# Spreading a bonus vector and loading weights without GpSimd, in a fused RWKV-6 and token-mixing kernel

## The chip, the cores and the metric

The kernel runs on one core of one Trainium2 chip. The metric is device time in microseconds. Before the change the median of three runs is 148.23 us (146.26 to 151.97).

## What is computed

Two stages follow each other. The first is a linear attention with a decaying state (batch 4, 8 heads, sequence 768, head size 48); the second mixes tokens with two projections and a last matrix product. Cut to what matters:

```python
for t in range(S):                       # S = 768, state is D x D per batch and head
    cur = einsum('bhd,bhe->bhde', u * k_t, v_t)      # u: the bonus vector, heads x D
    y_t = einsum('bhd,bhde->bhe', r_t, state + cur)
    state = w_t[..., None] * state + einsum('bhd,bhe->bhde', k_t, v_t)
x = y as (B, S, H*D)                     # H*D = 384
W_tok = (x @ w_q) @ (x @ w_k)^T / sqrt(64)
out = relu(W_tok @ x) @ w_out            # w_q, w_k: 384 x 64; w_out: 384 x 384
```

All inputs and the output are fp32.

## The kernel before

The sequence is cut into units ("tiles") of 256 tokens. There are 12: three for each of four batches, numbered n = 0 to 11. A tile holds 128 partitions with two tokens each, 8 heads and 48 elements. For each tile these steps are made (the name of the step is that of its function):

- `load` (L134, SP queue): w, k, r, v, 384 KB each, in three buffers per tensor.
- `log` (L139, ACT): logarithm of w. `sums` (PE): running sums of it by triangular matrices, into PSUM tiles `cw`. `expk` (L159, ACT) writes `em`, `expr` (L166, ACT) works on `cw` in place, `decay` (L173, ACT) writes `pt`.
- `rdec` (L182, DVE, two instructions) writes RdS = r times a decay. `kdec` (L189, POOL) writes KdS = k times `em`. `trR` transposes both on PE into `psT`; `evT` (L209, DVE) copies `psT` to RKT.
- `amat` (PE) and `mask` (L226, DVE, two instructions): the masked score matrix AmB.
- The bonus term is apart from it: `uk1` (L232, POOL) is k times `ubc`, the bonus vector u spread over all 128 partitions; `uk2` (L239, POOL) multiplies by r; `red` (L246, DVE) sums per head to `diag`; `vd` (L253, POOL) is V times `diag`; `vswap` (L260, SP queue) moves it into the token order of the output, Vn. `vcast` (L193, ACT) is the cast of v to V.
- `state`, `stadd` (PE), `stev` (L289, DVE): the state SB. `ymat`, `yst` (PE), `yev` (L325, DVE): X = Y + Vn.
- `xtr` (PE), `xev` (L341, ACT), `qkmat` (PE), `qkev` (L361 and L362, ACT): the projections of x.

After three tiles a batch is complete, and `tmat`, `tev` (L375), `mix`, `mixev` (L387), `fin`, `finev` (L404 on ACT, L406 on DVE) and `store` (L411, ACT queue) make its output. All matmuls are issued through one helper at L58.

The order of the work on each engine isn't left to a scheduler. Each step has a due time in a list (`steps`, and `bsteps` for a batch), tile n is displaced by n times P = 7.42, and all steps of all tiles are sorted by that time and written out in this order. Each engine works through its own part of it in order; an instruction that waits holds all behind it on its engine.

`uload` and `wload` are due first of all. `uload` (L450, L451) loads u into one partition over the SP queue, and GpSimd's partition broadcast spreads it to `ubc`. `wload` (L454 to L456) issues three transfers on GpSimd's queue: the query weights stay fp32 (`wq_f`), the key weights and the output weights are cast to bf16 by the transfer. `wcast` (L460, ACT) casts and scales the query weights after the first tiles' activations.

Of the kernel before, what the change touches and what calls it, by code (L numbers as in the profile page):

```python
# [11 lines left out]
F32 = mybir.dt.float32  # L12
# [6 lines left out]
def _rep(ap, axis, n):  # L19
    a = [list(x) for x in ap.ap]  # L20
    a.insert(axis, [0, n])
    return dataclasses.replace(ap, ap=a)
# [3 lines left out]
def kernel(  # L26
# [12 lines left out]
    nc = tc.nc  # L39
    B, H, S, D = r.shape  # L40
    C = 128
# [7 lines left out]
    DM = H * D  # L49
    DH = moe_w_q.shape[1]  # L50
    NK = DM // 128
# [15 lines left out]
    consts = ctx.enter_context(tc.tile_pool(name="consts", bufs=1))  # L67
# [14 lines left out]
            lst.append(consts.tile([C, 2, NP, C], BF16, name=f"{nm}{i}", tag=f"{nm}{i}"))  # L82
        PT.append(consts.tile([C, 2, H], F32, name=f"pt{i}", tag=f"pt{i}"))

    u1 = consts.tile([1, DM], F32, tag="u1")
    ubc = consts.tile([C, DM], F32, tag="ubc")
    wq_sb = consts.tile([128, NK, DH], BF16, tag="wq")
    wk_sb = consts.tile([128, NK, DH], BF16, tag="wk")
    wout_sb = consts.tile([128, NK, DM], BF16, tag="wo")
    wq_f = consts.tile([128, NK, DH], F32, tag="wqf")  # L90

    ld = ctx.enter_context(tc.tile_pool(name="ld", bufs=3))
    hw = ctx.enter_context(tc.tile_pool(name="hw", bufs=3))
# [24 lines left out]
    def at(t, fn):  # L118
        plan.append((t, len(plan), fn))
# [10 lines left out]
    def load(n, nm, ap):  # L130
        b, m = divmod(n, NU)
        src = ap[b, :, ds(m * C2, C2)]
        t = ld.tile([C, H, D2], F32, name=nm + "G", tag=nm + "G")
        nc.sync.dma_start(out=t, in_=src.rearrange("h (p j) d -> p h (j d)", j=2))  # L134
        T[nm, n] = t
# [311 lines left out]
        nc.vector.memset(PT[i], 0.0)  # L447

    def uload():
        nc.sync.dma_start(out=u1, in_=u.rearrange("h d -> (h d)"))  # L450
        nc.gpsimd.partition_broadcast(ubc, u1)  # L451

    def wload():
        nc.gpsimd.dma_start(out=wq_f, in_=moe_w_q.rearrange("(n p) h -> p n h", p=128))  # L454
        nc.gpsimd.dma_start(out=wk_sb, in_=moe_w_k.rearrange("(n p) h -> p n h", p=128))
        nc.gpsimd.dma_start(out=wout_sb, in_=moe_w_out.rearrange("(n p) d -> p n d", p=128))  # L456

    def wcast():
        T["wq"] = wq_sb
        nc.scalar.activation(wq_sb, wq_f, ACT.Copy, bias=0.0, scale=scale)  # L460

    P = 7.420616340685398
    steps = [
        (-6.28, log, ()),
        (2.72, uk1, ()),
        (2.75, uk2, ()),
        (3.11, sums, ()),
        (3.14, expk, ()),  # L470
        (3.14, expr, ()),
        (3.14, decay, ()),
        (4.39, rdec, ()),
        (6.88, kdec, ()),
        (8.86, vcast, ()),
        (9.54, trR, (0, )),
        (9.99, red, ()),
        (10.19, trR, (1, )),
        (10.98, evT, ()),
        (11.01, amat, (0, )),  # L480
        (12.45, mask, (0, )),
        (13.24, vd, ()),
        (13.27, vswap, ()),
        (14.3, amat, (1, )),
        (14.33, mask, (1, )),
        (16.24, state, ()),
        (16.65, stadd, (0, )),
        (16.68, stev, (0, )),
        (17.69, stadd, (1, )),
        (17.87, stev, (1, )),  # L490
        (17.98, ymat, ()),
        (18.01, yst, ()),
        (18.47, yev, ()),
        (20.81, xtr, ()),
        (22.26, xev, ()),
        (23.63, qkmat, ()),
        (24.22, qkev, ()),
    ]
    bsteps = [
        (-0.35, tmat, ()),  # L500
        (1.14, tev, ()),
        (2.14, mix, (0, )),
        (2.29, mixev, (0, )),
        (3.11, mix, (2, )),
        (3.65, mix, (1, )),
        (6.35, mixev, (1, )),
        (6.78, mixev, (2, )),
        (7.16, mix, (3, )),
        (8.18, mixev, (3, )),
        (9.78, mix, (5, )),  # L510
        (10.47, mixev, (5, )),
        (11.93, mix, (4, )),
        (11.97, mixev, (4, )),
        (12.0, fin, (0, )),
        (12.38, finev, (0, 0, )),
        (12.57, fin, (1, )),
        (12.76, finev, (1, 1, )),
        (14.6, store, (0, )),
        (15.74, fin, (2, )),
        (15.77, finev, (2, 0, )),  # L520
        (16.04, fin, (3, )),
        (16.1, fin, (5, )),
        (17.73, fin, (4, )),
        (17.82, finev, (4, 0, )),
        (18.28, finev, (3, 1, )),
        (19.09, finev, (5, 1, )),
        (19.92, store, (1, )),
        (20.86, store, (2, )),
    ]
    for n in range(NT):  # L530
        t0 = n * P
        tl = t0 - 3 * P + 9.67 if n >= 3 else n - 100
        for i, (nm, ap) in enumerate((("w", w), ("k", k), ("r", r), ("v", v))):
            at(tl + 0.01 * i, lambda n=n, nm=nm, ap=ap: load(n, nm, ap))
        for dt, fn, a in steps:
            if fn in (stadd, stev) and n % NU == NU - 1 and a == (1,):
                continue
            at(t0 + dt, lambda n=n, fn=fn, a=a: fn(n, *a))
        if n % NU == NU - 1:
            b = n // NU  # L540
            tb = t0 + 25.81
            for dt, fn, a in bsteps:
                at(tb + dt, lambda b=b, fn=fn, a=a: fn(b, *a))
    at(-99.995, uload)
    at(-98.995, wload)
    at(12.49573647335233, wcast)
    with tc.manual_schedule():
        for _, _, fn in sorted(plan, key=lambda x: x[:2]):
            fn()
# [30 lines left out]
```

## Time and profile before

The profile is of one execution on the chip.

| | |
|---|---|
| median of three runs | 148.23 us |
| the profiled execution's own time | 150.44 us |
| its span, first to last instruction | 148.7 us |
| busy: PE | 100.9 us (68%) |
| busy: DVE | 92.5 us (62%) |
| busy: POOL (GpSimd) | 88.1 us (59%) |
| busy: ACT | 81.8 us (55%) |
| moved by DMA | 26.66 MB, mean 179 GB/s |

PE is TensorE, PEld its weight loads, DVE VectorE, ACT ScalarE, POOL GpSimd, SP the engine that issues most transfers; a q behind a name (SPq, POOLq) is its issue of transfers. In a group such as `KdS<-kG,em`, the tile before the arrow is written from those behind it. The bracket at the end of a line of the timeline is the engine's idle time before it, and what ended it; "issue" means that the engine waited for nothing that the profile shows. The page divides the span into 40 equal slices of 3.7 us and gives for each the busy share of an engine in tenths.

### The profile page before, as it was taken

Reading aid. Unit: us, or ns where it says so; the run is one execution under the profiler, and the core shown is the slowest. Engines: PE = TensorE matmul, PEld = TensorE weight load, DVE = VectorE, ACT = ScalarE, POOL = GpSimd, SP = SyncE. Lnnn points to the kernel's source line nnn. Section 1 sums busy time; section 2 is a strip of 40 time slices with the busy share of each in tenths; the row PEclk is TensorE's granted clock in tenths of the full one; section 3 lists DMA queues with packets and bytes.
Section 4 is the critical chain, followed back from the end, with each engine's and each line's share of the span. In section 5 each row is a group of like instructions: output and inputs, shape, how many; then the busy total and the mean of one; then the engine's idle time right before and its main releaser. Section 6 shows DMA issues by size and latency. Waiting matters only on the chain. (4 is left out here: it accounts for less than half of the span.)

```text
span 148.7 us, 4118 instructions
## 1 busy us (share of the span) xinstructions
PE 100.9 (68%) x1684; PEld 66.7 (45%) x1684; DVE 92.5 (62%) x138; ACT 81.8 (55%) x174; POOL 88.1 (59%) x85
## 2 busy tenths in 40 slices
PE   0603000046797969689999899898989997986930
PEld 0202000033645746465767566464756564653410
DVE  5002000045769889898899896997989989760210
ACT  3235400008267376768897777498856782645520
POOL 7603400899999597989596987949596803000000
PEclk9999999999997899999999999999999999999695
DMA  4999990019298949679796967969856310248074
GB/s 115 298 270 309 309 194 0 0 26 293 60 281 231 321 127 285 182 193 271 188 235 173 324 181 226 296 173 246 221 134 166 109 40 4 53 110 212 0 198 119
DMA packets 58084, 26.66 MB, mean 179 GB/s; under 512 B 51505, under 2 KB 58034, under 8 KB 58066
## 3 DMA queue, kind: packets, MB, share of 16 engines
q1 hardware_dynamic: 53762, 21.24, 54.1%
q10 hardware_dynamic: 3456, 4.72, 11.6%
q0 software_dynamic: 848, 0.44, 2.0%
q8 instruction: 13, 0.21, 0.6%
q14 instruction: 5, 0.04, 0.1%
HBM read 19.66 MB, written 4.72 MB: 164 GB/s over the span
## 5 line engine op out<-in xcount | busy, mean ns | idle before, releaser
L159 ACT ACTIVATE em<-cw,bias 128x384 bf16<-128x384 f32 x24 | 12.8, 577 | 29.2 <-PE cw L58 29.2
L226 DVE TENSOR_TENSOR AmB<-A,MASK 128x1024 bf16<-128x1024 f32 x24 | 28.5, 1217 | 0.3 <-PE A L58 0.2
L253 POOL TENSOR_TENSOR Vd<-V,diag 128x768 bf16<-128x768 bf16 x12 | 17.7, 1474 | 17.9 <-DVE diag L246 12.8
L232 POOL TENSOR_TENSOR uk<-kG,ubc 128x768 f32<-128x768 f32 x12 | 21.7, 1809 | 9.6 <-issue 9.6
L239 POOL TENSOR_TENSOR uk<-uk,rG 128x768 f32<-128x768 f32 x12 | 21.7, 1810 | 0.9
L246 DVE TENSOR_REDUCE diag<-uk 128x16 f32<-128x768 f32 x12 | 11.3, 945 | 16.8 <-POOL uk L239 16.8
L58 PEld LDWEIGHTS <-KdS 64*128 64x128 bf16 (+1 forms) x256 | 11.6, 104 | 22.2 <-POOL KdS L189 17.7
L58 PE MATMUL psT<-ID,KdS 128*128 128x128 bf16 x96 | 8.3, 237 | 17.4 <-POOL KdS L189 17.4
L189 POOL TENSOR_TENSOR KdS<-kG,em 128x768 bf16<-128x768 f32 x12 | 19.6, 1636 | 0.3 <-ACT em L159 0.2
L182 DVE TENSOR_TENSOR RdS<-rG,cw 128x384 bf16<-128x384 f32 x24 | 12.1, 547 | 10.8 <-ACT cw L166 10.8
L58 PE MATMUL fps<-wout_sb,mixT 128*128 128x384 bf16 x72 | 15.4, 356 | 1.2 <-ACT osb L404 1.1
L139 ACT ACTIVATE logw<-wG 128x768 bf16<-128x768 f32 x12 | 10.1, 842 | 10.9 <-DMA wG<-in_w_dram 10.7
L325 DVE TENSOR_TENSOR X<-Y,Vn 128x768 bf16<-128x768 f32 x12 | 11.5, 958 | 7.3 <-PE Y L58 4.0
L209 DVE COPY RKT<-psT 128x2048 bf16<-128x2048 bf16 x12 | 14.6, 1216 | 1.7 <-PE psT L58 1.7
L58 PE MATMUL cw<-logw,BI 128*128 128x384 bf16 x36 | 11.4, 374 | 4.9 <-ACT logw L139 4.9
L58 PE MATMUL psT<-ID,RdS 128*128 128x128 bf16 x96 | 8.8, 241 | 7.6 <-DVE RdS L182 5.8
L289 DVE TENSOR_TENSOR SB<-Sn,pt 128x384 bf16<-128x384 f32 x20 | 11.1, 554 | 4.0 <-PE Sn L58 2.9
L387 ACT ACTIVATE mixT<-mps 128x384 bf16<-128x384 f32 x24 | 10.7, 493 | 4.6 <-PE mps L58 4.4
L341 ACT COPY XT<-xt_ps 128x768 bf16<-128x768 bf16 x12 | 9.6, 799 | 6.0 <-PE xt_ps L58 6.0
L58 PEld LDWEIGHTS <-RKT 48*64 48x64 bf16 (+1 forms) x464 | 10.3, 108 | 4.9 <-issue 2.6
L166 ACT ACTIVATE cw<-cw,bias 128x384 f32<-128x384 f32 x24 | 12.3, 558 | 0.2
L406 DVE COPY osb<-fps 128x384 f32<-128x384 f32 x12 | 6.6, 552 | 8.8 <-ACT mixT L387 5.0
(62 smaller groups left out, 172.3 us busy)
## 6 DMA issues: line engine op xcount, KB each, us to landing
wG<-in_w_dram SPq DMA_DIRECT2D x12, 384.0 KB, 5.0
kG<-in_k_dram SPq DMA_DIRECT2D x12, 384.0 KB, 5.2
rG<-in_r_dram SPq DMA_DIRECT2D x12, 384.0 KB, 5.6
vG<-in_v_dram SPq DMA_DIRECT2D x12, 384.0 KB, 5.8
out_dram<-osb ACTq DMA_DIRECT2D x24, 192.0 KB, 2.9
Vn<-Vd SPq DMA_DIRECT2D x48, 48.0 KB, 2.5
wout_sb<-in_moe_w_out_dram POOLq DMA_DIRECT2D x1, 288.0 KB, 6.6
wq_f<-in_moe_w_q_dram POOLq DMA_DIRECT2D x1, 96.0 KB, 5.1
```

Of the source, the lines that this page charges most:

```text
L58: nc.tensor.matmul(o, l, rr, start=start, stop=stop, skip_group_check=True, is_transpose=trans)
L159: nc.scalar.activation(em[:, j], T["cw", n, 1 + j][:, 0:DM], ACT.Exp, bias=bias[2 + j], scale=-1.0)
L166: nc.scalar.activation(cw, cw, ACT.Exp, bias=bias[j], scale=1.0)
L182: nc.vector.tensor_tensor(pad(Rd)[:, j], jhd(T["r", n])[:, j], T["cw", n, j][:, 0:DM].rearrange("p (h d) -> p h d", d=D), ALU.mult)
L189: nc.gpsimd.tensor_tensor(pad(T["Kd", n]), jhd(T["k", n]), hd(T["em", n]), ALU.mult)
L209: nc.vector.tensor_copy(RKT, T["psT", n])
L226: nc.vector.tensor_tensor(T["AmB", n][:, js].rearrange("p q h t -> p h q t"), T["A", n, js], _rep(_rep(MASK[:, js], 1, NP), 1, 2), ALU.mult)
L232: nc.gpsimd.tensor_tensor(uk, T["k", n].rearrange("p h (j d) -> p h j d", j=2), _rep(ubc.rearrange("p (h d) -> p h d", d=D), 2, 2), ALU.mult)
L239: nc.gpsimd.tensor_tensor(uk, uk, T["r", n].rearrange("p h (j d) -> p h j d", j=2), ALU.mult)
L246: nc.vector.tensor_reduce(diag.rearrange("p j h -> p h j"), T["uk", n], axis=AX.X, op=ALU.add)
L253: nc.gpsimd.tensor_tensor(Vd, T["V2", n], _rep(T["diag", n], 3, D), ALU.mult)
L325: nc.vector.tensor_tensor(T["X", b][:, ds(2 * m, 2)], T["Y", n][:, :, 0:DM], T["Vn", n], ALU.add)
```

## The change

The bonus vector is read by a transfer whose source repeats the 1536 bytes 128 times, so that it lands in all partitions; it is issued on the ACT queue ahead of the first `log`. The partition broadcast, and the one-partition tile u1, are gone. The three weights are loaded in fp32 on the ACT queue, due right after the first `log`, and ScalarE casts all three in `wcast`. The due times of nearly all steps are new; P is the same.

```diff
-    u1 = consts.tile([1, DM], F32, tag="u1")
+    wk_f = consts.tile([128, NK, DH], F32, tag="wkf")
+    wout_f = consts.tile([128, NK, DM], F32, tag="wof")
...
     def uload():
-        nc.sync.dma_start(out=u1, in_=u.rearrange("h d -> (h d)"))
-        nc.gpsimd.partition_broadcast(ubc, u1)
+        uf = u.rearrange("h d -> (h d)")
+        nc.scalar.dma_start(out=ubc, in_=_rep(uf, 0, C))

     def wload():
-        nc.gpsimd.dma_start(out=wq_f, in_=moe_w_q.rearrange("(n p) h -> p n h", p=128))
-        nc.gpsimd.dma_start(out=wk_sb, in_=moe_w_k.rearrange("(n p) h -> p n h", p=128))
-        nc.gpsimd.dma_start(out=wout_sb, in_=moe_w_out.rearrange("(n p) d -> p n d", p=128))
+        for t, a in ((wq_f, moe_w_q), (wk_f, moe_w_k), (wout_f, moe_w_out)):
+            nc.scalar.dma_start(out=t, in_=a.rearrange("(n p) h -> p n h", p=128))

     def wcast():
         T["wq"] = wq_sb
         nc.scalar.activation(wq_sb, wq_f, ACT.Copy, bias=0.0, scale=scale)
+        nc.scalar.copy(wk_sb, wk_f)
+        nc.scalar.copy(wout_sb, wout_f)
...
-        (-6.28, log, ()),
-        (2.72, uk1, ()),
-        (2.75, uk2, ()),
-        (3.11, sums, ()),
+        (-7.73, log, ()),
+        (-2.67, uk1, ()),
+        (1.48, sums, ()),
...
-        (6.88, kdec, ()),
-        (8.86, vcast, ()),
+        (4.93, uk2, ()),
+        (6.95, vcast, ()),
+        (7.29, kdec, ()),
...
-        (13.24, vd, ()),
-        (13.27, vswap, ()),
+        (12.04, vd, ()),
...
+        (14.71, vswap, ()),
...
-        tl = t0 - 3 * P + 9.67 if n >= 3 else n - 100
+        tl = t0 - 3 * P + 9.92 if n >= 3 else n - 100
...
-            tb = t0 + 25.81
+            tb = t0 + 24.41
...
-    at(-98.995, wload)
-    at(12.49573647335233, wcast)
+    at(-5.674325351920891, wload)
+    at(12.474566743711435, wcast)
```

On GpSimd this gives, for the first tiles, the order uk1(0), uk1(1), uk2(0), kdec(0), vd(0), uk1(2), uk2(1), kdec(1), vd(1), and so on; before it was uk1(0), uk2(0), kdec(0), uk1(1), uk2(1), vd(0), kdec(1), uk1(2), uk2(2), vd(1), kdec(2). The order of DVE's instructions is the same but for two swapped pairs of a mask and an output copy. On PE the `mix` and `fin` matmuls of a batch stand at other places between the tiles' matmuls. On ACT the `log` of a later tile and `vcast` change places.

More of the change, by code (lines that the diff above doesn't have):

```diff
@@ L460, in wcast @@
         nc.scalar.activation(wq_sb, wq_f, ACT.Copy, bias=0.0, scale=scale)
+        nc.scalar.copy(wk_sb, wk_f)
+        nc.scalar.copy(wout_sb, wout_f)
     P = 7.420616340685398
     steps = [
-        (-6.28, log, ()),
-        (2.72, uk1, ()),
-        (2.75, uk2, ()),
-        (3.11, sums, ()),
[L470 to L473, printed above, removed]
-        (6.88, kdec, ()),
-        (8.86, vcast, ()),
[L476 to L481, printed above, removed]
-        (13.24, vd, ()),
-        (13.27, vswap, ()),
[L484 to L497, printed above, removed]
+        (-7.73, log, ()),
+        (-2.67, uk1, ()),
+        (1.48, sums, ()),
+        (1.75, expk, ()),
+        (1.81, expr, ()),
+        (1.83, decay, ()),
+        (2.25, rdec, ()),
+        (4.93, uk2, ()),
+        (6.95, vcast, ()),
+        (7.29, kdec, ()),
+        (7.68, trR, (0, )),
+        (7.7, trR, (1, )),
+        (8.31, red, ()),
+        (8.67, evT, ()),
+        (9.5, amat, (0, )),
+        (11.63, mask, (0, )),
+        (12.04, vd, ()),
+        (12.63, amat, (1, )),
+        (12.66, mask, (1, )),
+        (14.53, state, ()),
+        (14.71, vswap, ()),
+        (14.96, stadd, (0, )),
+        (14.99, stev, (0, )),
+        (15.71, stadd, (1, )),
+        (15.74, stev, (1, )),
+        (16.59, ymat, ()),
+        (16.62, yst, ()),
+        (16.65, yev, ()),
+        (19.34, xtr, ()),
+        (19.87, xev, ()),
+        (21.93, qkmat, ()),
+        (22.64, qkev, ()),
     ]
@@ L500 @@
         (-0.35, tmat, ()),
-        (1.14, tev, ()),
+        (-0.32, tev, ()),
         (2.14, mix, (0, )),
-        (2.29, mixev, (0, )),
-        (3.11, mix, (2, )),
+        (2.33, mixev, (0, )),
         (3.65, mix, (1, )),
+        (4.58, mix, (2, )),
         (6.35, mixev, (1, )),
[L507 to L512, printed above, removed]
+        (6.64, mixev, (2, )),
+        (7.42, mix, (3, )),
+        (7.45, mixev, (3, )),
+        (9.08, mix, (5, )),
+        (9.81, mixev, (5, )),
+        (11.34, mix, (4, )),
         (11.97, mixev, (4, )),
-        (12.0, fin, (0, )),
-        (12.38, finev, (0, 0, )),
+        (12.34, fin, (0, )),
+        (12.37, finev, (0, 0, )),
         (12.57, fin, (1, )),
-        (12.76, finev, (1, 1, )),
+        (12.6, finev, (1, 1, )),
         (14.6, store, (0, )),
@@ L522 @@
         (16.1, fin, (5, )),
[L523 to L526, printed above, removed]
+        (17.36, finev, (3, 1, )),
+        (18.76, fin, (4, )),
+        (19.11, finev, (4, 0, )),
+        (19.14, finev, (5, 1, )),
         (19.92, store, (1, )),
```

## The prediction

> **What bounds the kernel now.** I read the page's 40 slices first. From slice 5 to 8 (18.6 to 31 us) every compute engine stands at or near 0, and afterwards DVE shows 8 or 9 to slice 34. So there are two stages: a start with a hole in it, and a steady run. The chain that ended last is of little use: it reaches back only to 134.8 us, the last matmuls and stores. So next come the stretches of time; columns are length, then busy time and count of each engine, TensorE clock, DMA share, GB/s.
>
> ```profile
> 6.40:13.60 7.20, 1.42 (x13) 0.54 (x11) 1.03 (x2) 3.14 (x7) 0.01 (x1) 1.00 1.07 286
> 13.60:16.80 3.20, 0.64 (x6) 0.37 (x4) 0.00 (x0) 1.56 (x2) 3.11 (x4) 1.00 1.17 321
> 16.80:26.40 9.60, 0.00 (x0) 0.00 (x0) 0.00 (x0) 0.00 (x0) 0.04 (x1) 1.00 0.62 130
> 26.40:31.00 4.60, 0.00 (x0) 0.00 (x0) 0.94 (x1) 0.00 (x0) 4.52 (x3) 1.00 0.00 0
> ...
> 66.00:131.00 65.00, 59.77 (x1127) 40.19 (x1124) 57.70 (x74) 48.03 (x106) 44.08 (x27) 1.00 0.67 179
> ```
>
> In 16.8 to 26.4 nothing computes. In 66 to 131 DVE is busy 57.70 of 65.00 us (89%), POOL 44.08: the steady run is DVE's. The timeline of POOL says what holds the start (start, duration, engine, line, operation, idle before it):
>
> ```profile
> 5.54 0.82 POOL L446 MEMSET KdS<- 128x256 bf16 x3
> 13.59 0.68 POOL L451 PARTITION_BROADCAST ubc<-u  x1 [7.24 <-issue]
> 14.12 1.06 POOL L454 DMA_DIRECT2D wq_f<-in_moe_w_q_dram  x1
> 15.20 0.78 POOL L455 DMA_DIRECT2D wk_sb<-in_moe_w_k_dram  x1
> 15.96 0.77 POOL L456 DMA_DIRECT2D wout_sb<-in_moe_w_out_dram  x1
> 26.36 1.79 POOL L232 TENSOR_TENSOR uk<-kG,ubc 128x768 f32<-128x768 f32 x1 [9.63 <-issue]
> 28.23 1.80 POOL L239 TENSOR_TENSOR uk<-uk,rG 128x768 f32<-128x768 f32 x1
> 29.99 1.63 POOL L189 TENSOR_TENSOR KdS<-kG,em 128x768 bf16<-128x768 f32 x1
> ```
>
> POOL is done with the constants at 6.36, and does its first tile work at 26.36. Both idle stretches (7.24 and 9.63 us) are "issue": no engine and no transfer ends them. Everything waits for the KdS of tile 0, as the waits say (total, times, longest):
>
> ```profile
> PEld L58 <- POOL KdS L189: 17.7, 1, 17.7
> PE psT L58 <- POOL KdS L189: 17.4, 1, 17.4
> DVE diag L246 <- POOL uk L239: 16.8, 1, 16.8
> POOL Vd L253 <- DVE diag L246: 12.8, 7, 5.1
> ```
>
> From KdS of tile 0 at 29.99 to the end are 118.7 us: DVE works tile after tile. KdS starts at 43.33 for tile 2 and 117.00 for tile 11: 73.67/9 = 8.19 us per tile. The page's DVE groups (AmB 28.5, RKT 14.6, RdS 12.1, X 11.5, diag 11.3, SB 11.1, osb 6.6) sum to 95.7 us, 7.98 per tile, so this is nearly all work. So a start earlier by d us should end earlier by nearly d, if the steady run keeps its 8.19.
>
> **What the change takes away.** The broadcast and three POOL-issued transfers, and with them both idle stretches, if these belong to them. Their instructions are 13.59 to 16.73, so 20.0 us (6.36 to 26.36) are POOL's to win at most. The Trainium skill (GPSIMD Engine Reference, Instruction dispatch) says that the first call of a freshly loaded GpSimd kernel pays about 6 us (5.95) that no instruction shows. The rows say 7.24 and 9.63, and I count by the rows. But the rule also speaks against the change: the first tensor operation after the constants could itself be such a first call. By the rule, uk of tile 0 would then start at 6.36+5.95 = 12.3, by the row at 6.36+9.63 = 16.0. The listing of the program has an extra GpSimd instruction ahead of the broadcast and another ahead of the first uk; the changed program has neither. So I take no such load, and keep 16.0 as a rival.
>
> **What then holds tile 0: transfers.** The start is bound by DMA. The log activations wait for w of tiles 0, 1 and 2:
>
> ```profile
> 4.05 0.84 ACT L139 ACTIVATE logw<-wG 128x768 bf16<-128x768 f32 x1 [2.04 <-DMA wG<-in_w_dram]
> 9.96 0.84 ACT L139 ACTIVATE logw<-wG 128x768 bf16<-128x768 f32 x1 [5.06 <-DMA wG<-in_w_dram]
> ...
> 15.12 0.84 ACT L139 ACTIVATE logw<-wG 128x768 bf16<-128x768 f32 x1 [2.01 <-DMA wG<-in_w_dram]
> ```
>
> Between w1 (9.96) and w2 (15.12) four loads of 393 KB land, so one per 1.29 us or 305 GB/s; k of tile 1 lands about 9.96+1.29 = 11.25 (estimate). The change puts on the ACT queue: ubc, 128 x 1536 B = 0.197 MB, before the first log; then q and k weights, 0.098 MB each, and the output weights, 0.590 MB, after it. That is 0.983 MB or 3.22 us at 305 GB/s. The whole of it could slip in ahead of k1, or only ubc (0.65 us). The Trainium skill (DMA: Bandwidth & Descriptors, Queues, rings and completion order) states that an engine takes queue rows in turn, packet by packet. The row here says only that the engines are full (share 1.07). By turns, weights issued from 4.9 us get half: 0.786 MB are through after about 1.57 MB in all, 5.2 us, at about 10.1, before k1. In one line behind SP's loads they would cost k1 nothing. I take turns: k1 lands at 11.25+3.22 = 14.5, w1 at 13.2.
>
> The changed order on POOL is uk1(0), uk1(1), uk2(0), kdec(0), vd(0): the second instruction needs k of tile 1 and stands ahead of tile 0's work. So uk1(1) starts at 14.5, uk2(0) at +1.87 (26.36 to 28.23), KdS(0) at +1.76 (28.23 to 29.99), so 18.1. Other inputs are there: log(1) at 13.2, em(0) 0.75 later and 1.04 long, so 15.0; ubc, issued by about 2.6 (table load over at 2.0, a transfer's issue 0.6), has until 14.5-1.87 = 12.6, where 5 us is the median landing of an SP load twice its size. **Gain at KdS(0): 29.99-18.1 = 11.9 us.** KdS(1) follows 6.7 later as before (29.99 to 36.65), since POOL then runs four operations back to back.
>
> **What is added on ACT.** Three issues after log(0) at 4.9: about 0.6 each as for the stores, 1.6 each if the queue is full like SP's (1.55). They lie in the 5.06 us before log(1), now longer; nothing is paid. Two more casts: 0.36 for wk (the wq row) and 0.81 x 1152/768 = 1.21 for wout, 1.57 us between pt(1) and V(1). ACT waited 3.47 us for cw(2) right behind that place (41.73), which hides them; without this cover they would cost 1.57 us once. V(1) then ends at 39.2 on the old clock; its first user Vd(1) can't start before diag(1), 40.15. The swap of log and V is inside the same wait. SP loses one issue of u (0.47): SP is backed up behind full engines, so nothing.
>
> **What is moved.** DVE's order is the same for all tiles but for two pairs of mask and osb swapped; PE's differs in where mix and fin matmuls stand, all moved inside waits of their batch. SP keeps its order. POOL's is what differs: before, vd(n) stood behind uk2(n+1) and kdec(n+1) just behind vd(n). Now vd(n) stands behind kdec(n), and uk1(n+2), uk2(n+1), kdec(n+1) stand behind it. Vd(n) waits for diag(n) on DVE. So KdS(n+1) is ready at diag(n)'s end +0.13+1.43+1.89+1.76+1.64 = 6.85 (steps between POOL's starts in the timeline). PE took up the KdS transposes of tiles 3 to 11 at 6.92, 6.59, 7.12, 6.82, 7.26, 7.79, 7.56, 7.39 and 7.01 after that end (57.19-50.27 for tile 3). It would be late by 0.26 at tile 4, 0.03 at tile 6, nothing else: 0.3 us, 0.5 with knock-on. Queued behind the transposes on PE are cw(n+2) and Y(n), and X(n) on DVE waits for Y. The loop diag(n), KdS(n+1), transposes, cw, Y, X(n), diag(n+2) is 6.85+0.45+1.27+1.05+5.48 = 15.1 us for two tiles, 7.6 a tile, under the 8.19.
>
> **Sum.** 148.7-11.9+0.5 = 137.3 span. The profiled execution took 150.44 for it, 1.74 around; the median 148.23 is 2.2 lower. From the median: 148.23-11.4 = **136.8 us**.
>
> **Rivals.**
> (a) As above: 136.8, chance 0.55.
> (b) The weights don't get in front of k1. It lands at 11.25+0.65 = 11.9, KdS(0) starts at 15.5, gain 14.5: 134.2. For it: SP has a long backlog. Against: two queues on full engines. 0.20.
> (c) The change doesn't clear POOL: the first uk still pays 9.63. uk1(0) at 16.0, uk1(1) 17.9, KdS(0) 21.5, gain 8.5: 140.2. For it: no row shows whose the "issue" time is. Against: the extra instructions are gone. 0.15.
> (d) The start is won, but moved ACT and PE steps cost about 1 us a tile in the steady run: 148.23-11.9+9 = 145.4, about no change. DVE's idle time there, 7.30 of 65 us in the stretch above, could double. 0.05.
> (e) The other side: the POOL loop becomes the bound. vd(n) behind kdec(n), waiting for DVE, holds KdS(n+1) and so PE and DVE. It decides when the loop is over 8.19+11.9/9 = 9.5 us a tile, 19.0 for two, against 15.1; at 10 us a tile the result is 148.23-11.9+9 x 1.81 = 152.6. For it: 12.8 us of Vd waiting for diag already. Against: four POOL operations at a steady 1.5 to 1.8 us would all have to grow by a quarter and more. 0.05.
>
> **Range.** Cases (a), (b), (c) hold 0.90; 133.0 to 140.8 reaches a little past (b) and (c) and leaves out (d), (e) and the edges. Measurement tells 2% from no change, so faster means under 145.3: 0.90; within 2% 0.05; slower 0.05.
>
> **What would show it.** POOL's first uk before 12 us and no "issue" idle of over 1 us; the second uk released by the DMA of k, near 14.5; KdS(0) near 18 (15.5 says (b), 21.5 says (c)); KdS from tile 2 to 11 at 8.1 to 8.3 us a tile; DVE still at 8 to 9. The prediction is wrong if KdS(0) starts after 25, or if the tile period moves by over 0.5 us.

## The result and the profile after

The changed kernel takes 138.69 us (median of 4 runs, 136.97 to 139.75) against 147.68 us (146.26 to 151.97) for the kernel before: a ratio of 0.934, 95% interval 0.917 to 0.952. Some executions of any of these kernels take over 1.5% longer than its fastest: the medians here are of all executions, the ratios are of means without these, and both profiled executions, before and after, are among the longer ones. In a second comparison, five rounds on another chip (y1 below), it took 137.6 us against 148.93, a ratio of 0.922 (0.914 to 0.929). The forecast was 136.8, range 133.0 to 140.8. The profiled execution took 139.31 us, with a span of 137.5; the forecast span was 137.3.

The stretches of time of the changed kernel (length, busy time of PE, PEld, DVE, ACT, POOL with counts, clock, DMA share, GB/s):

```profile
6.40:13.60 7.20, 2.29 (x14) 0.91 (x13) 0.00 (x0) 0.82 (x1) 1.80 (x1) 1.00 1.10 311
13.60:18.00 4.40, 0.85 (x7) 0.67 (x8) 1.02 (x2) 3.87 (x8) 2.73 (x2) 1.00 1.10 301
18.00:31.00 13.00, 8.66 (x96) 5.89 (x94) 7.89 (x10) 7.16 (x14) 10.90 (x8) 1.00 1.05 287
...
54.00:119.00 65.00, 59.83 (x1128) 39.85 (x1126) 58.10 (x75) 47.88 (x106) 45.97 (x28) 1.00 0.67 180
```

The hole in which nothing computed is gone: from 18 us on all engines work. What stands ahead of it now is DMA, with a share over 1 in all three rows. The 65 us of the steady run are those of before, moved: DVE is busy 58.10 us where it was 57.70, PE 59.83 where it was 59.77. POOL's timeline shows the start:

```profile
5.23 0.82 POOL L447 MEMSET KdS<- 128x256 bf16 x3
7.69 1.80 POOL L233 TENSOR_TENSOR uk<-kG,ubc 128x768 f32<-128x768 f32 x1 [1.64 <-DMA kG<-in_k_dram]
15.27 1.80 POOL L233 TENSOR_TENSOR uk<-kG,ubc 128x768 f32<-128x768 f32 x1 [5.78 <-DMA kG<-in_k_dram]
17.03 1.80 POOL L240 TENSOR_TENSOR uk<-uk,rG 128x768 f32<-128x768 f32 x1
18.80 1.63 POOL L190 TENSOR_TENSOR KdS<-kG,em 128x768 bf16<-128x768 f32 x1
20.39 1.47 POOL L254 TENSOR_TENSOR Vd<-V,diag 128x768 bf16<-128x768 bf16 x1
```

Both stretches that were ended by "issue" (7.24 and 9.63 us) are gone; the two left (1.64 and 5.78) have a name, the DMA of k. The second is uk1(1), waiting for k of tile 1 (k1) ahead of all of tile 0's other work. KdS(0) starts at 18.80 where it was 29.99, 11.2 us earlier. The last X of DVE starts at 119.59 where it was 130.82, also 11.2 earlier, and the span is 11.2 shorter: in this pair of profiles, what is won at the start is neither added to nor lost behind it. KdS starts at 34.06 for tile 2 and 107.77 for tile 11: 73.71/9 = 8.19 us per tile, as before. On ACT one thing was not forecast:

```profile
0.77 0.43 ACTq L452 DMA_DIRECT2D ubc<-in_u_dram  x1
6.38 0.84 ACT L140 ACTIVATE logw<-wG 128x768 bf16<-128x768 f32 x1 [4.36 <-DMA wG<-in_w_dram]
...
14.09 0.84 ACT L140 ACTIVATE logw<-wG 128x768 bf16<-128x768 f32 x1 [6.87 <-DMA wG<-in_w_dram]
```

The first log starts at 6.38, where it was 4.05: the repeating read, issued at 0.77, delays the very first load by 2.3 us (x6 below issues it later and has the log back at 4.18).

### The profile page after: what moved, and what is told of

It reads as the page before. It is cut to its first block, busy times and chain, and to the rows that moved or that the text cites. A ratio compares the mean times of both kernels' runs of the same rounds, so it can differ in the third digit from the quotient of the medians.

```text
span 137.5 us, 4126 instructions
## 1 busy us (share of the span) xinstructions
PE 100.8 (73%) x1684; PEld 66.2 (48%) x1684; DVE 92.4 (67%) x138; ACT 83.1 (60%) x176; POOL 84.5 (61%) x81
## 5 line engine op out<-in xcount | busy, mean ns | idle before, releaser
L58 PE MATMUL fps<-wout_sb,mixT 128*128 128x384 bf16 x72 | 15.9, 357 | 1.2 <-ACT osb L405 1.1
L58 PE MATMUL cw<-logw,BI 128*128 128x384 bf16 x36 | 11.4, 374 | 7.3 <-ACT logw L140 7.3
L58 PEld LDWEIGHTS <-RdS 128*128 128x128 bf16 x96 | 7.1, 108 | 11.2 <-DVE RdS L183 8.5
```

The costliest lines, as they stand in the source:

```text
L58: nc.tensor.matmul(o, l, rr, start=start, stop=stop, skip_group_check=True, is_transpose=trans)
```

## The experiments

The theory: the gain is POOL's cleared start; the idle belongs to the broadcast; the new start is bound by k1, which the weights and the bonus read push back; and the order of the steps gives nothing. The main rival: it is the new order that makes the kernel faster, or GpSimd's own transfers that made the holes. Labels with x ran in two groups of four, those with y in a third; each group has its own runs of the kernel before. KdS(0) is the start of tile 0's KdS in the profile.

| label | what it is | KdS(0), us | span, us | median, us | ratio to before (95%) |
|---|---|---|---|---|---|
| x1 | new loads, old order | 15.67 | 132.8 | 135.26 | 0.909 (0.905 to 0.914) |
| x2 | old loads, new order | 30.82 | 150.3 | 151.96 | 1.020 (1.015 to 1.025) |
| x3 | only the broadcast back | 29.03 | 145.4 | 148.54 | 0.999 (0.995 to 1.003) |
| x4 | only the weights back on GpSimd | 18.97 | 135.5 | 137.36 | 0.921 (0.915 to 0.927) |
| x5 | weights issued a log later | 16.37 | 135.5 | 137.22 | 0.928 (0.912 to 0.943) |
| x6 | bonus read issued after the first log | 18.11 | 135.6 | 137.47 | 0.930 (0.919 to 0.940) |
| x7 | distinct rows in place of the bonus row | 16.97 | 136.7 | 138.56 (one run) | - |
| x8 | x1 with late bonus read and late weights | 13.29 | 135.3 | 137.06 (134.34 to 138.60) | - |
| y1 | the changed kernel again | 18.45 | 135.6 | 137.6 | 0.922 (0.914 to 0.929) |
| y2 | x1 with late bonus read | 13.80 | 136.9 | 136.46 | 0.915 (0.909 to 0.922) |
| y3 | changed kernel, first stores written out later | 19.08 | 138.0 | 140.87 | 0.948 (0.941 to 0.954) |

**x1, the old order with the new loads.** The loads, casts and places of `wload` and `wcast` of the change are put into the kernel before; its list of steps stays.

```diff
-    at(-98.995, wload)
+    at(-5.674325351920891, wload)      # uload, wload, wcast as in the change; steps as before
```

> The new loads with the old order of the steps. Theory (the whole gain is POOL's cleared start, and the new order costs or gives nothing in the steady run): without uk1(1) ahead of it, KdS(0) waits only for em(0), which stood at 15.9 us in the changed kernel, so KdS(0) starts near 16 instead of 18.8, and the span is about 134.7 (137.5 less 2.8). Rival (the new order is what brings the gain, or is needed for it): KdS(0) early or not, the tile period is over 8.5 us and the span 140 or more.

POOL's timeline of x1:

```profile
9.54 1.80 POOL L240 TENSOR_TENSOR uk<-uk,rG 128x768 f32<-128x768 f32 x1
15.67 1.64 POOL L190 TENSOR_TENSOR KdS<-kG,em 128x768 bf16<-128x768 f32 x1 [4.34 <-ACT em L160]
17.26 1.81 POOL L233 TENSOR_TENSOR uk<-kG,ubc 128x768 f32<-128x768 f32 x1
```

uk1(1) stands behind KdS(0) here, so KdS(0) waits for `em` alone and starts at 15.67. From KdS of tile 2 (29.31) to tile 11 (102.07) are 72.76/9 = 8.08 us per tile. The old order needs nothing of the new one, and the new loads alone make the whole gain and nearly 2 us more (0.909 against 0.921 for x4 in the same group, and 0.922 for y1). No kernel here has a lower ratio.

**x2, the new order with the old loads.** `uload`, `wload` and `wcast` are those of before, in the changed list.

```diff
-    at(-5.674325351920891, wload)
+    at(-98.995, wload)                 # uload, wload, wcast as before; steps as in the change
```

> The new order of the steps with the old loads: broadcast and three transfers on GpSimd. Theory: both idle stretches of 7.24 and 9.63 us are back, the first uk starts at 26.4, uk1(1) stands ahead of uk2(0), so KdS(0) starts at 31.8 and the span is about 150.5 (148.7 plus 1.8). Rival (the order matters by itself): span under 146.

Idle stretches of 7.01 and 9.01 us are back, KdS(0) starts at 30.82 and the span is 150.3. The order alone makes the kernel 2% slower (1.5 to 2.5%). One more POOL operation stands ahead of KdS(0), which starts 0.8 us later than before; another 1.0 us is lost between X(5) and X(6) (10.64 us apart, 9.68 before), where X(6) waits 2.51 us for Vn, a wait that y3 below comes back to. The rival that the order makes the gain falls.

**x3, only the broadcast back.**

```diff
-        nc.scalar.dma_start(out=ubc, in_=_rep(uf, 0, C))
+        nc.sync.dma_start(out=u1, in_=u.rearrange("h d -> (h d)"))
+        nc.gpsimd.partition_broadcast(ubc, u1)
```

> The changed kernel with only the bonus vector back on GpSimd's broadcast; weights stay on the ACT queue. Theory (both idle stretches belong to the broadcast, one ahead of it and one at the next tensor operation): broadcast at 13.6, first uk at 14.1 plus 9.6 = 23.8, KdS(0) at 29.3, span about 148. Rival (the second stretch belongs to the transfers that GpSimd issued): first uk at 14.1, KdS(0) at about 19.6, span about 138.5.

**x4, only the weights back on GpSimd's queue.** `ubc` is still spread by the transfer.

```diff
-        for t, a in ((wq_f, moe_w_q), (wk_f, moe_w_k), (wout_f, moe_w_out)):
-            nc.scalar.dma_start(out=t, in_=a.rearrange("(n p) h -> p n h", p=128))
+        nc.gpsimd.dma_start(out=wq_f, in_=moe_w_q.rearrange("(n p) h -> p n h", p=128))
+        nc.gpsimd.dma_start(out=wk_sb, in_=moe_w_k.rearrange("(n p) h -> p n h", p=128))
+        nc.gpsimd.dma_start(out=wout_sb, in_=moe_w_out.rearrange("(n p) d -> p n d", p=128))
```

> The changed kernel with only the weights back on GpSimd's queue; the bonus vector is spread by the repeating read. Theory (the idle belongs to the broadcast): GpSimd issues its three transfers in 2.6 us after 6.05, the first uk starts at 8.7, no idle of 7 us, KdS(0) within 1 us of 18.8 or earlier as the transfers move fewer bytes, span 136 to 138.5. Rival (the second stretch belongs to GpSimd's transfers): first uk at 8.7 plus 9.6 = 18.3, KdS(0) at about 23.8, span about 142.5.

The timelines of POOL, first of x3, then of x4:

```profile
5.54 0.82 POOL L448 MEMSET KdS<- 128x256 bf16 x3
15.29 0.68 POOL L453 PARTITION_BROADCAST ubc<-u  x1 [8.92 <-DMA rG<-in_r_dram]
23.75 3.55 POOL L234 TENSOR_TENSOR uk<-kG,ubc 128x768 f32<-128x768 f32 x2 [7.78 <-issue]
```

```profile
6.01 0.93 POOL L453 DMA_DIRECT2D wq_f<-in_moe_w_q_dram  x1
6.94 0.76 POOL L454 DMA_DIRECT2D wk_sb<-in_moe_w_k_dram  x1
7.70 0.77 POOL L455 DMA_DIRECT2D wout_sb<-in_moe_w_out_dram  x1
8.54 1.80 POOL L231 TENSOR_TENSOR uk<-kG,ubc 128x768 f32<-128x768 f32 x1
```

With one broadcast and none of the transfers, POOL idles 8.92 us ahead of it and 7.78 behind it, and the whole gain is gone: the time is that of before to within 0.5%. With the three transfers and no broadcast, the first uk follows 0.07 us after the last issue. So the broadcast owns both stretches, and it alone made the 8%. (The first stretch of x3 is put down to the DMA of r, which the broadcast doesn't need; that landing is only the last event before its end. Nor is it a wait for u: the semaphore of u's transfer was full at 4.05 us in the kernel before and at 3.95 in x3, ahead of both stretches.)

What stands just ahead of each stretch is in the views of the lines L451 and L232 of the kernel before (count, ns of one, first and last start):

```profile
L451 POOLq MODIFY_POOL_CONFIG  x2: 22/22/22, 6.3 to 6.3; - x2
L232 POOLq MODIFY_POOL_CONFIG  x2: 37/37/37, 16.8 to 16.8; - x2
```

POOL executes a pair of these instructions at 6.3 us, then nothing till the broadcast at 13.59; another pair at 16.8, then nothing till the first uk at 26.36. x2 and x3 have both pairs in the same places (6.3 and 15.9 us in x3). The changed kernel and all others without the broadcast have neither. A first pair, at 1.0 to 1.3 us in every kernel, is followed by no such stretch, so the instruction by itself isn't the cost; what POOL does in the two stretches no run here takes apart.

The three transfers lie under the wait for k1, and taking them off GpSimd is worth nothing that these runs can see.

**x5, the weights a log later.**

```diff
-    at(-5.674325351920891, wload)
+    at(-0.3, wload)
```

> The changed kernel with the three weight transfers issued right after the second log instead of the first. Theory (the weights take turns with the loads of SP and so pushed w1 and k1 back by their 0.786 MB at 305 GB/s, 2.6 us): the second log starts at 11.5 instead of 14.1, uk1(1) at 12.7 instead of 15.3, KdS(0) at 16.3 instead of 18.8, and the time falls by about 2.5 us. Rival (the weights slip in behind SP's loads and cost k1 nothing): uk1(1) stays at 15.3 and the time is the changed kernel's.

The lines of x5 on POOL (uk1(1), KdS(0), and the uk of tile 2) are these:

```profile
12.84 1.80 POOL L233 TENSOR_TENSOR uk<-kG,ubc 128x768 f32<-128x768 f32 x1 [3.42 <-DMA kG<-in_k_dram]
...
16.37 1.63 POOL L190 TENSOR_TENSOR KdS<-kG,em 128x768 bf16<-128x768 f32 x1
...
20.81 1.81 POOL L233 TENSOR_TENSOR uk<-kG,ubc 128x768 f32<-128x768 f32 x1 [1.37 <-DMA kG<-in_k_dram]
```

The second log starts at 11.61 (14.09 in the changed kernel), uk1(1) at 12.84 (15.27), KdS(0) at 16.37 (18.80): the weights do get in among SP's loads, and cost 2.4 to 2.5 us there, as worked out (2.6). But the time does not fall; the ratio is that of the changed kernel within its interval (plus or minus 1.6%, so a gain of 1 us could hide in it, the 2.5 that were forecast hardly). Part of the bytes are only moved: k2 (k of tile 2) is late now, and uk of tile 2 waits 1.37 us for it. Against y1, KdS(0) is 2.1 us ahead, KdS(1) 0.65, X(0) 1.0 (30.71 to 31.70), and X(1) 0.1 behind (39.38 to 39.28). The last microsecond goes with PE's clock: the trace of x5 records it at half from 33.41 to 36.82 us, that of y1 has no such stretch there. In all 13 profiles, X(1) starts 8.61 to 8.73 us behind X(0) where a stretch at half lies between them (eight of them), and 7.58 or 7.59 where none does (five). The first profile of the changed kernel has one in the same place, and against it x5 is still 1.4 us ahead at X(11). So single profiles don't say whether anything is left at the end; the times show nothing.

**x6, the bonus read after the first log.**

```diff
-    at(-99.995, uload)
+    at(-5.7, uload)
```

> The changed kernel with the repeating read of the bonus vector issued after the first log, ahead of the weights. Theory (the start of tile 0's first log at 6.4 instead of 4.1 is due to this read, but only k1 counts): first log back at 4.1, second log still at 13 to 14.1 as all bytes are still ahead of it, KdS(0) at 18 to 18.8, time within 1 us of the changed kernel. Rival (the lost 2.3 us at the start are lost for good): second log at 11.8, KdS(0) at 16.5, 2.3 us faster.

The first log is back at 4.18, the second starts at 11.78, which I had not expected; but uk1(1) waits for k1 till 14.59 and KdS(0) starts at 18.11, and the time is the changed kernel's. In this order the landing of k1 sets the start of KdS(0), not the log.

**x7, distinct rows in place of one row read 128 times.** The bonus vector's tile gets 128 rows of the output weights.

```diff
-        nc.scalar.dma_start(out=ubc, in_=_rep(uf, 0, C))
+        nc.scalar.dma_start(out=ubc, in_=moe_w_out[0:C])
```

> The changed kernel in which the transfer into ubc reads 128 different rows of 1536 bytes (of the output weights) instead of one row 128 times; so the bonus term is computed with other numbers in place of u. Theory (reading one row 128 times is slower than its bytes): ubc lands in 4 us or less instead of 5.0, first log at about 4.8 instead of 6.4, second log at 13.1 instead of 14.1. Rival (any second queue at the start costs this): 6.4 and 14.1 again.

The same bytes land in 3.5 us instead of 5.0, the first log starts at 4.88 instead of 6.38, and uk1(1) at 13.44 instead of 15.27. Reading one 1536-byte row for all partitions is slower than its bytes here, and holds the loads beside it by about 1.5 us (one execution; y1 has 6.01 and 14.92 in place of 6.38 and 15.27, so 1.1 to 1.5 at the log and 1.5 to 1.8 at uk1(1)). The second log came earlier (10.77) than was forecast (13.1): w of tile 1 landed ahead of the output weights here (10.75 and 12.35) and behind them in the changed kernel (14.07 and 13.82). How two queues share the engines differs from run to run.

**x8 and y2, the start made as early as it gets.** x8 is x1 with the bonus read after the first log and the weights after the second; y2 is x1 with the late bonus read alone.

```diff
-    at(-99.995, uload)
-    at(-5.674325351920891, wload)
+    at(-6.2, uload)
+    at(1.15, wload)                    # x8 only
```

> The new loads with the old order of the steps, the bonus read issued after the first log and the weights after the second. Theory (all terms at the start add up): first log at 4.1, second at 11.6, em(0) done at 13.4, KdS(0) at 13.7, which is 2 us ahead of the old order with the new loads (15.7), and a span of about 130.8. Rival (with KdS(0) so early, later loads hold the next tiles, since all bytes are only moved behind): KdS(0) at 13.7, but KdS(2) at 29 again and the span at 132.8.

> The new loads with the old order of the steps, and only the bonus read issued after the first log (the weights behind it, ahead of the second log). Theory (what holds KdS(0) in the old order is em(0), behind the second log): second log at 11.8 as with the late bonus read in the new order, em(0) done at 13.6, KdS(0) at 13.7 instead of 15.7, span 131 to 132 and 1 to 2 us faster than with the old order alone. Rival (a tile or two later nothing is left of it, as with the late weights): time within 0.5 us of the old order with the new loads, ratio 0.905 to 0.912 to the kernel before.

KdS(0) starts at 13.29 and 13.80, 1.9 to 2.4 us ahead of x1, as forecast, and no gain over x1 is seen: y2's ratio is 0.915 (a little above the rival's 0.905 to 0.912, which its interval covers), and of x8's four executions the shortest took 134.34 us, where x1's took 134.62. The rivals fit better than the theories. (The spans of y2 and x8 in the table are of executions of 138.71 and 137.12 us, that of x1 is of one of 134.62.) In y2 X(5) starts at 69.56 where x1 has 69.46: by then nothing is left. Then a wait stands out in DVE's timeline of y2:

```profile
81.58 0.96 DVE L326 TENSOR_TENSOR X<-Y,Vn 128x768 bf16<-128x768 f32 x1 [3.87 <-DMA Vn<-Vd]
```

X(6) waits 3.86 us for Vn in x8 too, 2.41 in y1, 0.94 in x1. This is where most of x1's lead over y1 comes from (2.8 us at KdS(0), but only 0.9 at X(5); 2.3 at X(6), 2.1 at X(11)).

**y3, the first stores written out later.** SP's waits in the changed kernel name the cause of that wait (total, times, longest):

```profile
SPq L261 <- DMA out_dram<-osb: 6.4, 3, 5.3
```

Vd of tile 6 is done at 72.5, and its transfer is issued at 76.94: SP waits for a store of the output on ACT's queue, which it doesn't need. In the trace the first transfer of Vn and a store issued at 72.52 use one semaphore (102); the store filled it at 76.87, and the transfer was issued 0.07 us later.

```diff
-        (14.6, store, (0, )),
+        (20.0, store, (0, )),
...
-        (19.92, store, (1, )),
+        (20.01, store, (1, )),
```

> The changed kernel with the first two stores of each batch written out later, behind the Vn transfers of the tile in work. Theory (SP's Vn transfer of tile 6 is ready at 72.5 and issued at 76.9 because it waits for a store on the ACT queue, and DVE loses 1.9 us in X(6)): the Vn transfer of tile 6 is issued within 1 us of its Vd, X(6) waits under 0.5 us for it, the time falls by 1 to 3 us over three batches. Rival (the stores only wait for SP's transfers instead, or X(6) waits for something else just as long): time within 1 us of the changed kernel.

Vn of tile 6 is moved by four transfers. The first is now issued at 71.30, right behind its Vd, but the fourth still waits for a store:

```profile
SPq L261 <- DMA out_dram<-osb: 2.8, 1, 2.8
77.01 0.46 SPq L261 DMA_DIRECT2D Vn<-Vd  x1
```

It shares its semaphore with a store that filled it at 76.99. In y1 the four are issued from 75.75 to 78.49. So the edit shortened the wait and did not take it away. X(6) starts only 0.24 us earlier (80.64 to 80.88 in y1), and the wait that ends last there is now 1.57 us for PE. At X(11) the two kernels are level (118.00 and 117.97). All of the loss, 2.4 us of span, comes behind that, where the stores crowd: the last six stand in one row from 130.51 for 4.06 us, where y1 has four from 129.42 for 2.62. Both expectations fail. What X(6) and the end would gain from a Vn that waits for no store at all stays untested.

**y1, the changed kernel again.**

> The changed kernel itself, timed beside the others on one chip and profiled once more. Theory: the tile period is the one of before, 8.1 to 8.3 us, KdS(0) at 18.8, and the ratio to the kernel before is 0.92 to 0.93. It also shows how much of the distance between single profiles (spans of 137.5, 135.5 and 135.6 for the changed kernel, the late weights and the late bonus read) is scatter: if its span is 135 to 136, all of it.

Its span is 135.6, 1.9 less than in the first profile, with KdS(0) at 18.45 and 72.43/9 = 8.05 us per tile (33.72 to 106.15). The clock rows of the two profiles, the first one's and y1's:

```profile
PEclk9999999999689999999999999999999999999595
```

```profile
PEclk9999999999999999999999999999999999999595
```

The first has a dip to 0.6 and 0.8 in two slices: in the trace the clock is at half from 35.27 to 38.68 us, between X(0) and X(1). The first profile is 0.35 us behind y1 at KdS(0), 1.1 at X(0) and 2.2 at X(1). So a single profile scatters by 2 us, and spans of x5, x6 and the changed kernel are not to be told apart.

## Why the prediction was right

- **The hole.** Both idle stretches went with the broadcast. The prediction allowed them to belong to its transfers too ("if these belong to them"); x3 and x4 show that they are the broadcast's alone. What the Trainium skill (GPSIMD Engine Reference, Instruction dispatch) states of the first call of a freshly loaded GpSimd kernel, about 6 us without a visible instruction, is the nearest rule and too small: 7.0 to 8.9 us ahead of the broadcast and 7.8 to 9.6 behind it in the kernels that have it. The extra instructions that the prediction went by are the two pairs in the views above. No tensor operation of the changed kernel paid such a stretch, so rival (c) is out.
- **What holds tile 0.** The chain w1, k1, uk1(1), uk2(0), KdS(0) is the one in the trace. uk1(1) started at 15.27, not 14.5, KdS(0) at 18.80, not 18.1. That the weights get ahead of k1 is shown by x5; this was the choice between (a) and (b). The terms can be read from the semaphores of the traces: k1 landed at 11.39 us before (11.25 estimated), at 12.77 in x5, with the bonus read but not the weights ahead of it, and at 15.20 in the changed kernel. So the weights cost 2.4 us (2.6 counted), and the bonus read 1.4, where its bytes gave 0.65: that is the error of 0.7. x7 points the same way: as many distinct rows cost less.
- **ACT.** The issues took 0.48 to 0.51 us (0.6), the casts 0.34 and 1.15 (0.36 and 1.21), and ACT still waited 2.15 us for the next cw (of tile 2): hidden, as said.
- **The moved steps.** 0.5 us were counted for KdS coming late to PE. After tile 0 the trace has one such wait, 0.22 us for KdS(4), where 0.26 was forecast, and the period is 8.19 as before; both profiles have one stretch at half clock in the first batch, and y1, without it, has 8.05. The order is not without a price, though: x1 is nearly 2 us faster without it. At the start it holds KdS(0) for k1, 3.1 us (x1), which the prediction had in the sum as given, without saying that the order before did not have it; and X(6) waits for Vn, 1.9 to 2.4 us, which the prediction did not have.
- **The sum.** Gain at KdS(0) 11.2 (11.9), steady run 0 (0.5 lost), together 11.2 (11.4). That the two misses cancel is luck. So is part of the rule that a start earlier by d ends earlier by nearly d: it held for the 11.2 us of this pair, but not for the 2 us by which x5, x8 and y2 were earlier still. The prediction took it from DVE groups that sum to 7.98 us per tile of 8.19; but neighbours overlap there (95.7 us against 92.5 in DVE's own row), and the stretch of 65 us has DVE busy 89%, so there was more slack than it read.

## What to carry to other kernels

Here an idle stretch just ahead of an instruction of another kind on GpSimd, and again just behind it, was the price of that one instruction: a broadcast of 0.68 us cost some 17 us of waiting, and a transfer that does the same put k1 back by 1.4. The view of the line shows what else the engine executed there. Look for such holes at the start, where no steady work covers them. And once the hole is closed, follow the first tile's chain, but measure the end: moving bytes about in this start, which DMA bounds, brought KdS(0) forward by 0.3 to 2.4 us (x5, x6, x8, y2), and the time by nothing that these runs can see.

## What was not expected of the hardware

- A transfer that reads one row of 1536 bytes 128 times took 5.0 us and one of as many distinct rows 3.5, and the load beside it came 1.5 us later (x7).
- The pair of prefix-sum matmuls takes 0.84 us in the first tiles and 0.49 later, though the clock row stands at its highest in both. The row is no witness there: the trace has clock records only from 29.77 us on in y1 and from 31.86 in the first profile, and ahead of the first record the page shows the highest digit all the same. Where there are records, the matmuls follow them. In x4 the clock is at half from 27.94 to 31.35 us (a row of stretches, then the pair inside and behind that stretch):

```profile
27.94:31.35 3.41, 3.41 (x30) 2.56 (x30) 2.51 (x4) 0.58 (x1) 2.09 (x2) 0.50 0.72 181
30.41 0.85 PE L58 MATMUL cw<-logw,BI 128*128 128x384 bf16 x2
38.20 0.49 PE L58 MATMUL cw<-logw,BI 128*128 128x384 bf16 x2
```

From one matmul of 384 columns to the next it is 0.320 us at half clock and 0.163 at full (medians in the eleven profiles that have at least three of each). Ahead of the first record it is 0.320 too, and in y1 the step comes at 29.6 to 29.9 us, where its records begin. So the early matmuls ran at the pace of the half clock; that the clock itself stood at half there is the likely reading, and not recorded. What sets the moment, which differs by 2 us between two profiles of one kernel, stays open.
